# Pooled attention by head: scores in quarters of the PE, products with V in blocks of 48 queries

## The chip, the cores and the metric

The kernel runs on one core of a Trainium2 chip. The metric is the device time of one execution in microseconds; a kernel is timed in several runs, and the median stands for it. The engines of a core are PE (matrix products, results in eight banks of PSUM), DVE (vector work), ACT (scalar functions and copies), POOL, and SP, which here only issues DMAs.

## The reference

Attention in two branches, then a feed-forward network (FFN). All inputs are float32; B = 8 batches, H = 8 heads, S = 576 positions, D = 64.

```python
q_d = q.reshape(B, H, Sd, factor, D).mean(axis=3)      # factor 4, Sd = 144; k_d, v_d alike
out_d = sm_attn(q_d, k_d, v_d)                         # softmax(scale * q k^T) v, the pooled branch
out_up = np.repeat(out_d, factor, axis=2)
mask = np.abs(pos[:, None] - pos[None, :]) < factor    # the local branch: 3 neighbours to each side
...
out_local = np.matmul(attn, v)
x = out_up + out_local                                 # (B, S, 512)
...
xn = (x - mu) / np.sqrt(var + 1e-06) * g_ln
out = x + np.maximum(xn @ w_ch1, 0.0) @ w_ch2          # 512 -> 2048 -> 512
```

The change lies in the pooled branch: for each batch and head, 144 pooled queries against 144 pooled keys, of 64 numbers each.

## The kernel before

**Tiling.** The FFN goes through the 8 x 576 = 4608 rows in 18 chunks of 256, each in 8 parts (`ffn`): line 1048 multiplies up into `h`, line 1071 multiplies down into `acc`, with ACT (`hh`) and DVE (`hl`) between. Each float32 operand there is a sum of two rounded halves, so that one product is three matmuls in the fast float32 form. The attention products are plain float32: each matmul leaves two records in the profile, a turn (transpose) one.

**Local branch** (`local`): windows of 58 rows; scores at lines 573 and 587 in 64x64 quarters of the PE, weights turned at line 622, products with V at line 643 in quarters too.

**Pooled branch** (`pooled_half`, `pooled_pair`): for each batch two halves of four heads, in each two pairs of heads (`pr`); 32 pairs in all. The first batch's pairs (`own`, `b < NPB`) get their pooled queries and keys from another path (`own_half`, line 428 turns them; `arrange`); the other 28 pairs go through `turn_qk`. A pair takes these steps, whose tile names the profile shows:

- `turn_qk` (line 791, PE, tile `gq`): the two heads' pooled queries and keys, 72 groups at a time, are turned so that the 2 x 64 numbers of the heads lie on 128 partitions.
- `turn_qk_out` (lines 800 and 804, ACT): the queries are copied into `qbdg`, a block-diagonal tile: for each block of 48 queries 96 columns, head 0's in the upper 64 partitions and head 1's in the lower, zeros elsewhere. The keys go to `ktg` as they are.
- `scores` (line 818, PE, `gs`): three matmuls, one for each block of 48 queries; thanks to the zeros one matmul does both heads, 96 rows of scores.
- `largest` (lines 822 and 823, DVE, `gmx`) and `exps` (line 831, ACT, `ag`): softmax's maximum and exponentials, three of 96x144.
- `turn_a` (line 837, PE, `gt`): the weights are turned, two tasks (`kh`, halves of 72 keys) of three turns; `turn_a_out` (line 847, ACT, `agt`) puts them in order by head.
- `times_v` (line 854, PE, `gv`): eight matmuls of 72 queries by 65 columns (V and a column of ones, whose product is softmax's sum), accumulated over the key halves.
- `divided` (lines 861 to 871, DVE) and `keep` (line 877, SP): division, and one DMA for the pair into `ud` in DRAM, from where the rows come back repeated (`load_up`).

**What sets the order.** Nothing is scheduled on the chip. Every step is a task of `Plan` with an engine, an assumed duration, the tasks it waits for, a due time, and what it takes and gives back: work units of SBUF ("u", 88 of them), PSUM banks ("a", 8) and staging buffers. `Plan.order` plays the tasks through with these numbers and writes the instructions of each engine in the order that results; on the chip each engine works through its list in that order. `CHUNK` is the planner's assumed pace of a chunk, and the due times of all branches hang on it. So attention work of later batches stands in PE's list between FFN groups, and an assumed duration changes the order alone.

Of the kernel before, what the change touches and what calls it, by code (L numbers as in the profile page):

```python
# [9 lines left out]
F32 = mybir.dt.float32  # L10
# [3 lines left out]
AF = mybir.ActivationFunctionType  # L14
# [125 lines left out]
def attention_then_ffn(  # L140
# [72 lines left out]
    qbdg = [const.tile([P, 3, 2 * GB], F32, name=f"qbdg{i}") for i in range(2)]  # L213
# [3 lines left out]
    for t in qbdg:  # L217
        nc.vector.memset(t, 0.0)
# [54 lines left out]
    CHUNK = 56  # L273
# [459 lines left out]

    def pooled_half(b, hg):
# [44 lines left out]
    def pooled_pair(b, hg, pr, x, ready):  # L779
# [5 lines left out]
        bd, vd = qbdg[pr], vds[hg]  # L785
# [11 lines left out]
        def turn_qk_out():  # L797
            for h2 in range(2):
                hs = slice(64 * h2, 64 * h2 + 64)
                nc.scalar.copy(  # L800
                    bd[hs, :, h2 * GB : (h2 + 1) * GB], y.pt[hs, 0].rearrange("p (c g) -> p c g", c=3)
                )
            y.kt = work.tile([P, SD], F32, tag="ktg", bufs=2, name=f"ktg{i}_{pr}")
            nc.scalar.copy(y.kt, y.pt[:, 1])

        def arrange():
            for h2 in range(2):
                hs = slice(64 * h2, 64 * h2 + 64)
                nc.scalar.copy(
                    bd[hs, :, h2 * GB : (h2 + 1) * GB],  # L810
                    gsum[b, hg, "q"][hs, pr].rearrange("p (c g) -> p c g", c=3),
                )
            y.kt = gsum[b, hg, "k"][:, pr]

        def scores():
            y.ps = psa(f"gs{i}_{pr}")[: 2 * GB, : 3 * SD].rearrange("p (c g) -> p c g", c=3)
            for c in range(3):
                nc.tensor.matmul(y.ps[:, c], lhsT=bd[:, c], rhs=y.kt, start=True, stop=True)  # L818
# [23 lines left out]
        def turn_a_out(kh):  # L842
            if own:
                y.at[kh] = unit([GH, 2, SD], f"agt{i}_{pr}_{kh}")
            else:
                y.at[kh] = work.tile([GH, 2, SD], F32, tag=f"agt{kh}", name=f"agt{i}_{pr}_{kh}")
            nc.scalar.copy(y.at[kh].rearrange("p h (c g) -> p c h g", c=3), y.pa[kh])

        def times_v():
            y.pv = psa(f"gv{i}_{pr}")[:GH, : 4 * (D + 1)].rearrange("p (q h e) -> p q h e", q=2, h=2)  # L850
            for h2 in range(2):
                for qh in range(2):
                    for kh in range(2):
# [3 lines left out]
                        )  # L857

# [23 lines left out]
        if b < NPB:  # L882
            t = add("ACT", 0.43, arrange, ready["q"] + ready["k"] + [lastg.s[pr]], due - 8.0)
# [3 lines left out]
        t = lastg.s[pr] = add(  # L887
            "PE", 0.73, scores, (t,), due - 6.0, take=A, give=(("u", 2),) if b < NPB and pr else ()
        )
        t = add("DVE", 0.7, largest, (t,), due - 5.0)  # L890
        ex = add("ACT", 0.79, exps, (t, None if own else lastg.t), due - 5.0, take=U if own else (), give=A)
        outs = []
        for kh in range(2):
            t = lastg.t = add("PE", 0.25, lambda kh=kh: turn_a(kh), (ex,), due - 3.0, take=A,
                                give=U if own and kh else ())
            outs.append(add("ACT", act(288), lambda kh=kh: turn_a_out(kh), (t, None if own else lastg.v), due - 3.0,
                            take=U if own else (), give=A))
        t = add("PE", 1.04, times_v, outs + ready["v"], due - 1.0, take=A, give=(("u", 2),) if own else ())
        lastg.v = lastg.vd[hg] = t
        t = add("DVE", 0.68, divided, (t,), due, take=U if b < NPB and pr == 0 else (), give=A)  # L900
        od_done.append(t)
        t = add("SP", 0.42, keep, (t,), due, lag=LAT)
# [208 lines left out]
    plan.add("POOL", 2.5, make_masks, (), 0.0)  # L1111
    choice_done = plan.add("POOL", 4.0, make_choice, (), 10.0, take=U)
# [58 lines left out]
```

## Time and profile before

| what | value |
|---|---|
| median of 3 runs | 1056.92 us (1055.81 to 1063.01) |
| the profiled execution | 1053.27 us, span 1051.3 us |
| granted PE clock, mean | 0.995 |
| PE, records of pooled scores (line 818) | 192, the first at 17.3 us, the last at 872.8 us |
| PE, records of turned weights (line 837) | 192, 24.6 to 877.3 us |
| PE, records of products with V (line 854) | 512, 30.7 to 879.8 us |
| longest wait in all, ACT `hh` for PE `h` | 363.5 us in 102 waits |
| waits of PE of over 1 us in all | `gt` for ACT `ag` 3.2, `lv` for ACT `at` 2.2, `gs` for ACT `ktg` 1.6, `gs` for DVE `hl` 1.4, `lt` for ACT `la` 1.2, and 1.5 at the start |

How to read it: a row of the profile names the line, the engine, the operation, then out<-in by the program's tile names, and the shapes. For a matmul `96*72` means 96 rows (the contraction) and 72 columns of weights, and the shape behind it what streams through, as partitions x columns. "PEld" are weight loads, which the profile lists apart. Durations of matmuls are modelled up to their end and overlap one another; the starts are what the hardware recorded.

### The profile page before, as it was taken

The numbers are of one execution on the slowest core, as the hardware profiler recorded it, in microseconds if no ns is written. First come the engines' busy times: TensorE is split into PE (matmuls) and PEld (weight loads), VectorE is DVE, ScalarE is ACT, GpSimd is POOL, SyncE is SP. The second block draws the span as 40 slices with busy tenths as digits, with TensorE's granted clock in tenths as the row PEclk, the third lists the DMA queues.
The fourth block names the chain that finished last, engine by engine and source line by source line (L and its number), as shares of the span: only waits on it lengthen the run. The fifth ranks groups of instructions, "written<-read, shape, count | busy, mean of one in ns | idle before, by whom it ended". The sixth has DMA issues, their size and how long they took to land.

```text
span 1051.3 us, 24104 instructions
## 1 busy us (share of the span) xinstructions
PE 1034.3 (98%) x9450; PEld 928.9 (88%) x9450; DVE 514.0 (49%) x1301; ACT 309.8 (29%) x846; POOL 251.0 (24%) x272
## 2 busy tenths in 40 slices
PE   9999899999999999999999999999999999999998
PEld 8887798988899989989898989899989899888997
DVE  7799976343444435444434443544434444534211
ACT  6676533232212222221323222222221222221110
POOL 4213552214014320231404150141401300000000
PEclk9999999999999999999999999999999999999999
DMA  7897474434344534343434443253442443301000
GB/s 177 251 283 210 136 176 95 114 64 114 61 101 91 133 75 110 62 124 56 91 94 96 104 97 99 47 134 67 114 87 69 92 88 65 80 11 52 7 21 21
DMA packets 283702, 104.38 MB, mean 99 GB/s; under 512 B 229789, under 2 KB 270493, under 8 KB 283589
## 3 DMA queue, kind: packets, MB, share of 16 engines
q1 hardware_dynamic: 283589, 102.84, 40.8%
q8 instruction: 75, 1.23, 0.5%
q14 instruction: 38, 0.31, 0.1%
HBM read 82.58 MB, written 11.80 MB: 90 GB/s over the span
## 4 chain that ended last, share of the span: by engine, by line
PE 83%; DVE 6%; DMA 5%; SPq 2%; issue 1%; POOL 1%; ACT 1%; ACTq 0%; DVEq 0%; POOLq 0%
PE h L1048 34%; PE acc L1071 33%; PE gv L854 3%; DMA s<-in_moe_w_ch_dram 2%; PE gs L818 2%; PE lv L643 2%; PE ls L587 2%; DVE cva L370 2%; PE lt L622 1%; PE px L975 1%; PE gt L837 1%; DVE lo L383 1%; SPq L714 1%; DMA x<-xl 1%; DVE cva L367 1%
## 5 line engine op out<-in xcount | busy, mean ns | idle before, releaser
L1071 PE MATMUL acc<-hi,hl 128*128 128x512 f32 x576 | 237.2, 412 | 0.6 <-DVE hl L1059 0.5
L1071 PE MATMUL acc<-lo,hh 128*128 128x512 f32 x576 | 227.4, 395 | 0.0
L1071 PE MATMUL acc<-hi,hh 128*128 128x512 f32 x576 | 225.2, 391 | 0.0
L1059 DVE SCALAR_TENSOR_TENSOR hl<-h,hh 128x512 fp32r<-128x512 f32 x144 | 98.9, 687 | 250.7 <-ACT hh L1055 222.0
L1055 ACT ACTIVATE hh<-h 128x512 fp32r<-128x512 f32 x144 | 86.2, 599 | 430.3 <-PE h L1048 363.5
L1048 PE MATMUL h<-xh,lo 128*128 128x256 f32 x1152 | 193.6, 291 | 0.2 <-DVE lo L383 0.2
L1048 PE MATMUL h<-xh,hi 128*128 128x256 f32 x1152 | 185.2, 283 | 0.0
L1048 PE MATMUL h<-xlo,hi 128*128 128x256 f32 x1152 | 185.0, 283 | 0.0
L1048 PEld LDWEIGHTS h<-xh,lo 128*128 128x128 f32 x1152 | 169.0, 190 | 17.4 <-DVE lo L383 0.4
L1048 PEld LDWEIGHTS h<-xlo,hi 128*128 128x128 f32 x1152 | 158.9, 192 | 0.0
L1048 PEld LDWEIGHTS h<-xh,hi 128*128 128x128 f32 x1152 | 158.6, 191 | 0.0
L948 POOL TENSOR_TENSOR x<-x,up 128x512 f32<-128x512 f32 x32 | 41.2, 1287 | 386.3 <-DMA x<-xl 208.1
L1071 PEld LDWEIGHTS acc<-hi,hh 128*128 128x128 f32 x576 | 108.5, 188 | 25.0
L1071 PEld LDWEIGHTS acc<-hi,hl 128*128 128x128 f32 x576 | 109.2, 190 | 16.9 <-DVE hl L1059 1.2
L1071 PEld LDWEIGHTS acc<-lo,hh 128*128 128x128 f32 x576 | 109.5, 190 | 12.7 <-DVE lo L383 0.3
L982 ACT ACTIVATE xh<-px,gain 128x128 fp32r<-128x128 f32 x144 | 43.7, 372 | 72.7 <-PE px L975 42.4
L992 DVE SCALAR_TENSOR_TENSOR xlo<-px,gain,xh 128x128 fp32r<-128x128 f32 x144 | 43.1, 345 | 39.1 <-ACT xh L982 38.6
L1079 DVE SCALAR_TENSOR_TENSOR x<-acc,x 128x512 f32<-128x512 f32 x36 | 24.7, 689 | 39.8 <-PE acc L1071 39.8
L831 ACT ACTIVATE ag<-gs,gmx 96x144 f32<-96x144 f32 x96 | 29.0, 374 | 41.9 <-DVE gmx L823 34.4
L370 DVE SCALAR_TENSOR_TENSOR cva<-s,cva 128x256 int32<-128x256 int32 x64 | 40.0, 665 | 1.1
L854 PEld LDWEIGHTS gv<-vd,agt 72*72 72x72 f32 x512 | 37.1, 145 | 1.2
L854 PE MATMUL gv<-vd,agt 72*72 72x65 f32 x512 | 37.9, 228 | 0.0
(196 smaller groups left out, 1106.9 us busy)
## 6 DMA issues: line engine op xcount, KB each, us to landing
s<-in_moe_w_ch_dram SPq DMA_DIRECT2D x64, 256.0 KB
vwin<-in_v_dram SPq DMA_DIRECT2D x160, 64.0 KB
out_dram<-x SPq DMA_DIRECT2D x36, 256.0 KB
qr<-in_q_dram SPq DMA_DIRECT2D x264, 32.0 KB
kr<-in_k_dram SPq DMA_DIRECT2D x264, 32.0 KB
up<-ud SPq DMA_DIRECT2D x28, 256.0 KB
x<-xl SPq DMA_DIRECT2D x74, 42.0 KB
ud<-od SPq DMA_DIRECT2D x32, 72.0 KB
```

Source lines behind the costliest of these rows:

```text
L370: nc.vector.scalar_tensor_tensor(out=a, in0=x.raw[i].rearrange("p (n two) -> p n two", two=2)[:, :, 0], scalar=29, in1=a, op0=ALU.logical_ ...
L587: nc.tensor.matmul(x.ps[par][64 * h2 : 64 * h2 + 64, pr], lhsT=x.qt[hs, 2 * pr + h2], rhs=x.kt[hs, 2 * pr + h2], start=True, stop=True,)
L831: nc.scalar.activation(y.a[:, c], y.ps[:, c], AF.Exp, scale=POOLED_SCALE, bias=y.mx[:, c : c + 1])
L854: nc.tensor.matmul(y.pv[:, qh, h2], lhsT=y.at[kh][:, h2, qh * GH : (qh + 1) * GH], rhs=vd[:, kh, 2 * pr + h2], start=kh == 0, stop=kh == 1,)
L948: nc.gpsimd.tensor_add(xt[n], xt[n], x.up)
L982: nc.scalar.activation(xh[c][i][:, k, j * P : (j + 1) * P], pxt[n][:, kc], AF.Copy, scale=gain[:, kc : kc + 1])
L992: nc.vector.scalar_tensor_tensor(out=xlo[c][i][:, k, ts], in0=pxt[n][:, kc], scalar=gain[:, kc : kc + 1], in1=xh[c][i][:, k, ts].bitcast(F ...
L1048: nc.tensor.matmul(ph[c, p][:, fi], lhsT=wt[:, kc], rhs=xx[kc // 2][:, kc % 2], start=n == 0, stop=n == 3 * KC - 1)
L1055: nc.scalar.activation(hh[c, p], ph[c, p], AF.Relu)
L1059: nc.vector.scalar_tensor_tensor(out=hl[c, p].rearrange("p c t -> p (c t)"), in0=ph[c, p].rearrange("p c t -> p (c t)"), scalar=0.0, in1=h ...
L1071: nc.tensor.matmul(acc[c][j], lhsT=lt[:, fi, ts], rhs=rt, start=p == 0 and fi == 0 and n == 0, stop=p == NPR - 1 and fi == 1 and n == 2,)
L1079: nc.vector.scalar_tensor_tensor(out=x, in0=acc[c][j], scalar=1.0 + 2.0**-23, in1=x, op0=ALU.mult, op1=ALU.add)
```

## The change

For the 28 pairs outside the first batch the block-diagonal tile goes. The queries and keys of the pair are copied out together (`turn_qk_out_both`, one copy of 288 columns). Scores are made head by head (`scores_by_head`): for each of three blocks of 48 queries one matmul for each head, head 0 in the PE quarter at rows 0 and columns 0, head 1 in that at rows 64 and columns 64, each head with a PSUM bank of its own. Maximum, exponentials, turns and the copies behind them run once for each head (`largest_by_head`, `exps_by_head`, `turn_a_by_head`, `turn_a_out_by_head`), on 48 partitions at 0 or at 64. The turns of a head use the PE rows 0 to 63 or 64 to 127, all columns. The products with V (`times_v_by_third`) go by thirds of 48 queries, with head 0's results in the left column half and head 1's in the right: for head 0 64 columns of weights are loaded (the 48 and 16 of the next block), so that rows 48 to 63 of the result hold numbers too. `divided_by_third` divides 112 partitions by 3 blocks, and `keep_by_third` stores the pair with two DMAs.

The first batch keeps the old way. Its two block-diagonal tiles are no longer constants but two of the 88 work units, cleared on DVE by a task of their own and given back behind the first batch's scores. The planner's numbers for the new tasks are in the diff, and `CHUNK` is 55 instead of 56.

```diff
-    qbdg = [const.tile([P, 3, 2 * GB], F32, name=f"qbdg{i}") for i in range(2)]
+    qbdg = []
...
-    for t in qbdg:
-        nc.vector.memset(t, 0.0)
...
-    CHUNK = 56
+    CHUNK = 55
...
+    def clear_qbdg():
+        for pr in range(2):
+            qbdg.append(unit([P, 512], f"qbdg{pr}")[:, : 6 * GB].rearrange("p (c g) -> p c g", c=3))
+            nc.vector.memset(qbdg[pr], 0.0)
...
-        def turn_qk_out():
-            for h2 in range(2):
-                hs = slice(64 * h2, 64 * h2 + 64)
-                nc.scalar.copy(
-                    bd[hs, :, h2 * GB : (h2 + 1) * GB], y.pt[hs, 0].rearrange("p (c g) -> p c g", c=3)
-                )
-            y.kt = work.tile([P, SD], F32, tag="ktg", bufs=2, name=f"ktg{i}_{pr}")
-            nc.scalar.copy(y.kt, y.pt[:, 1])
+        def turn_qk_out_both():
+            y.qk = work.tile([P, 2, SD], F32, tag="ktg", bufs=2, name=f"ktg{i}_{pr}")
+            nc.scalar.copy(y.qk.rearrange("p t g -> p (t g)"), y.pt.rearrange("p t g -> p (t g)"))
+
+        def scores_by_head():
+
+            y.ps = [psa(f"gs{i}_{pr}_{h2}")[:, : 3 * SD].rearrange("p (c g) -> p c g", c=3) for h2 in range(2)]
+            for c in range(3):
+                for h2 in range(2):
+                    hs = slice(64 * h2, 64 * h2 + 64)
+                    nc.tensor.matmul(
+                        y.ps[h2][64 * h2 : 64 * h2 + GB, c], lhsT=y.qk[hs, 0, c * GB : (c + 1) * GB], rhs=y.qk[hs, 1],
+                        start=True, stop=True,
+                    )
+
+        def largest_by_head(h2):
+            hs = slice(64 * h2, 64 * h2 + GB)
+            if h2 == 0:
+                y.mx = work.tile([64 + GB, 3], F32, tag="gmx", bufs=4, name=f"gmx{i}_{pr}")
+            nc.vector.reduce_max(y.mx[hs], y.ps[h2][hs], axis=AX.X)
+            nc.vector.tensor_single_scalar(out=y.mx[hs], in_=y.mx[hs], scalar=-POOLED_SCALE, op=ALU.mult)
+
+        def exps_by_head(h2):
+            hs = slice(64 * h2, 64 * h2 + GB)
...
+            for c in range(3):
+                nc.scalar.activation(
+                    y.a[hs, c], y.ps[h2][hs, c], AF.Exp, scale=POOLED_SCALE, bias=y.mx[hs, c : c + 1]
+                )
+
+        def turn_a_by_head(h2):
+            hs = slice(64 * h2, 64 * h2 + GB)
+            y.pa = getattr(y, "pa", {})
+            y.pa[h2] = psa(f"gt{i}_{pr}_{h2}")[:GH, : 6 * GB]
+            for kh in range(2):
+                for c in range(3):
+                    n = (3 * kh + c) * GB
+                    nc.tensor.transpose(
+                        y.pa[h2][:, n : n + GB], y.a[hs, c, kh * GH : (kh + 1) * GH], ident[hs, hs]
+                    )
...
+        def times_v_by_third():
+
+
+            y.pv = psa(f"gv{i}_{pr}")[: 64 + GB, : 3 * (D + 1)].rearrange("p (c e) -> p c e", c=3)
+            for c in range(3):
+                for kh in range(2):
+                    for h2 in range(2):
+                        m = GB if h2 else 64
+                        c0 = (6 * h2 + 3 * kh + c) * GB
+                        nc.tensor.matmul(
+                            y.pv[64 * h2 : 64 * h2 + m, c], lhsT=y.at.rearrange("p h n -> p (h n)")[:, c0 : c0 + m], rhs=vd[:, kh, 2 * pr + h2],
+                            start=kh == 0, stop=kh == 1,
+                        )
...
-            t = add("ACT", 0.52, turn_qk_out, (t, lastg.s[pr]), due - 8.0, give=A)
+            t = add("ACT", 0.36, turn_qk_out_both, (t, lastg.qk.get(pr)), due - 8.0, give=A)
...
+            t = lastg.qk[pr] = add("PE", 0.4, scores_by_head, (t,), due - 6.0, take=(("a", 2),))
+            exs = []
+            for h2 in range(2):
+                t1 = add("DVE", 0.78, lambda h2=h2: largest_by_head(h2), (t,), due - 5.0)
+                exs.append(add("ACT", 1.1, lambda h2=h2: exps_by_head(h2), [t1, lastg.t] + exs, due - 5.0, give=A))
...
-        t = add("PE", 1.04, times_v, outs + ready["v"], due - 1.0, take=A, give=(("u", 2),) if own else ())
+        t = add("PE", 1.04 if own else 0.5, times_v if own else times_v_by_third, outs + ready["v"], due - 1.0, take=A, give=(("u", 2),) if own else ())
```

What this does to the order is shown at three places in PE's list, for the second pair of the first half of batch 3, counted from 0 (6_1 in the names). First the scores. Before:

```order
L1071 MATMUL acc4_1_4473<-lo2_4_1597,hh4_2_4483 128x512
L1071 MATMUL acc4_1_4473<-hi2_4_1575,hh4_2_4483 128x512
L818 MATMUL gs6_1_4642<-ktg6_1_4620,qbdg1_81 96x144 x3
L1071 MATMUL acc4_0_4472<-hi2_5_1603,hl4_2_4498 128x512
L1071 MATMUL acc4_0_4472<-lo2_5_1644,hh4_2_4483 128x512
```

and now, up to the first of the three matmuls for each head:

```order
L1123 MATMUL h4_4_4718<-xh4_1_4340,hi1_9_1839 128x256 x2
L1123 MATMUL h4_4_4718<-xlo4_0_4351,hi1_9_1839 128x256 x2
L1123 MATMUL h4_4_4718<-xlo4_1_4364,hi1_9_1839 128x256 x2
L810 MATMUL gs6_1_0_4795<-ktg6_1_4770 48x144
L810 MATMUL gs6_1_1_4796<-ktg6_1_4770 48x144
```

Three matmuls of 96 rows in one bank have become six of 48, alternating between the heads and their banks; they still stand between FFN groups. The turns of the weights, before:

```order
L622 MATMUL lt13_4685<-ident_66,la13_4654 128x128 x4
L837 MATMUL gt6_1_0_4690<-ident_66,ag6_1_4679 72x96 x3
L837 MATMUL gt6_1_1_4694<-ident_66,ag6_1_4679 72x96 x3
L1048 MATMUL h4_5_4664<-xh4_0_4175,lo1_11_2048 128x256 x2
L1048 MATMUL h4_5_4664<-xh4_1_4185,lo1_11_2048 128x256 x2
```

and now (`lt` and `lv` belong to the local branch):

```order
L620 MATMUL lt13_4863<-ident_66,la13_4851 128x128 x4
L838 MATMUL gt6_1_0_4870<-ident_66,ag6_1_4837 72x48 x6
L1123 MATMUL h4_5_4822<-xh4_0_4328,lo1_11_2096 128x256 x2
L1123 MATMUL h4_5_4822<-xh4_1_4340,lo1_11_2096 128x256 x2
L1123 MATMUL h4_5_4822<-xh4_0_4328,hi1_11_2071 128x256 x2
L1123 MATMUL h4_5_4822<-xh4_1_4340,hi1_11_2071 128x256 x2
L1123 MATMUL h4_5_4822<-xlo4_0_4351,hi1_11_2071 128x256 x2
L1123 MATMUL h4_5_4822<-xlo4_1_4364,hi1_11_2071 128x256 x2
L838 MATMUL gt6_1_1_4893<-ident_66,ag6_1_4837 72x48 x6
L641 MATMUL lv13_0_4900<-vwin1_77,at13_4889 64x65 x2
```

The two tasks of turns, which waited for the same exponentials and stood side by side, wait for a head's each; here an FFN group stands between them, as in 13 of the 28 pairs. The products with V, before, with the first two of eight matmuls:

```order
L1048 MATMUL h4_5_4664<-xh4_1_4185,hi1_11_1998 128x256 x2
L1048 MATMUL h4_5_4664<-xlo4_0_4192,hi1_11_1998 128x256 x2
L1048 MATMUL h4_5_4664<-xlo4_1_4209,hi1_11_1998 128x256 x2
L854 MATMUL gv6_1_4718<-vd0_82,agt6_1_0_4710 72x65
L854 MATMUL gv6_1_4718<-vd0_82,agt6_1_1_4714 72x65
```

and now, with the first two of twelve:

```order
L1146 MATMUL acc4_1_4554<-hi2_6_1780,hl4_3_4733 128x512
L1146 MATMUL acc4_1_4554<-lo2_6_1798,hh4_3_4716 128x512
L1146 MATMUL acc4_1_4554<-hi2_6_1780,hh4_3_4716 128x512
L906 MATMUL gv6_1_4933<-vd0_80,agt6_1_4891 64x65
L906 MATMUL gv6_1_4933<-vd0_80,agt6_1_4891 48x65
```

They too stay between FFN groups, now as alternating matmuls of 64 and 48 queries.

More of the change, by code (lines that the diff above doesn't have):

```diff
@@ L784, in pooled_pair @@
         own = b < NPB
-        bd, vd = qbdg[pr], vds[hg]
+        vd = vds[hg]
         def turn_qk():
@@ L806, in arrange, with turn_a_out_by_head @@
+        def turn_a_out_by_head(h2):
+            if h2 == 0:
+                y.at = work.tile([GH, 2, 6 * GB], F32, tag="agt", name=f"agt{i}_{pr}")
+            nc.scalar.copy(y.at[:, h2], y.pa[h2])
         def arrange():
@@ L817, in scores @@
             for c in range(3):
-                nc.tensor.matmul(y.ps[:, c], lhsT=bd[:, c], rhs=y.kt, start=True, stop=True)
+                nc.tensor.matmul(y.ps[:, c], lhsT=qbdg[pr][:, c], rhs=y.kt, start=True, stop=True)
         def largest():
@@ L842, in turn_a_out @@
         def turn_a_out(kh):
[L843 to L846, printed above, removed]
+            y.at[kh] = unit([GH, 2, SD], f"agt{i}_{pr}_{kh}")
             nc.scalar.copy(y.at[kh].rearrange("p h (c g) -> p c h g", c=3), y.pa[kh])
@@ L857, in times_v, with divided_by_third, keep_by_third @@
                         )
+        def times_v_by_third():
[9 more added lines that the diff above has]
+                        )
+        def divided_by_third():
+            r = work.tile([64 + GB, 3], F32, tag="gr", bufs=4, name=f"gr{i}_{pr}")
+            nc.vector.tensor_scalar(
+                out=r, in0=y.pv[:, :, D], scalar1=1e-9, scalar2=float(FACTOR), op0=ALU.add, op1=ALU.mult
+            )
+            nc.vector.reciprocal(r, r)
+            y.od = work.tile([64 + GB, 3, D], F32, tag="od", bufs=2, name=f"od{i}_{pr}")
+            nc.vector.tensor_mul(y.od, y.pv[:, :, :D], r.unsqueeze(2).broadcast_to([64 + GB, 3, D]))
+        def keep_by_third():
+            if b not in ud:
+                ud[b] = dram.tile([SD, DM], F32, tag="ud", name=f"ud{b}")
+            for h2 in range(2):
+                c0 = (4 * hg + 2 * pr + h2) * D
+                nc.sync.dma_start(
+                    ud[b].rearrange("(c g) e -> g c e", c=3)[:, :, c0 : c0 + D], y.od[64 * h2 : 64 * h2 + GB]
+                )
         def divided():
@@ L882, in pooled_pair @@
         if b < NPB:
[L883 removed]
+            t = add("ACT", 0.43, arrange, ready["q"] + ready["k"] + [lastg.s[pr], bd_done], due - 8.0)
         else:
             t = add("PE", 0.25, turn_qk, ready["q"] + ready["k"], due - 8.0, take=A, give=(("u", 2),) if pr else ())
[L886 to L889 removed]
@@ L890, in pooled_pair @@
-        t = add("DVE", 0.7, largest, (t,), due - 5.0)
-        ex = add("ACT", 0.79, exps, (t, None if own else lastg.t), due - 5.0, take=U if own else (), give=A)
+            t = add("ACT", 0.36, turn_qk_out_both, (t, lastg.qk.get(pr)), due - 8.0, give=A)
+        if own:
+            t = lastg.s[pr] = add("PE", 0.73, scores, (t,), due - 6.0, take=A, give=(("u", (2 if pr else 0) + hg),) if pr or hg else ())
+            t = add("DVE", 0.7, largest, (t,), due - 5.0)
+            exs = [add("ACT", 0.79, exps, (t,), due - 5.0, take=U, give=A)]
+        else:
+            t = lastg.qk[pr] = add("PE", 0.4, scores_by_head, (t,), due - 6.0, take=(("a", 2),))
+            exs = []
+            for h2 in range(2):
+                t1 = add("DVE", 0.78, lambda h2=h2: largest_by_head(h2), (t,), due - 5.0)
+                exs.append(add("ACT", 1.1, lambda h2=h2: exps_by_head(h2), [t1, lastg.t] + exs, due - 5.0, give=A))
@@ L1111, in attention_then_ffn @@
     plan.add("POOL", 2.5, make_masks, (), 0.0)
+    bd_done = plan.add("DVE", 0.6, clear_qbdg, (), 0.0, take=(("u", 2),))
     choice_done = plan.add("POOL", 4.0, make_choice, (), 10.0, take=U)
```

12 lines of the change are left out of this document (7 added, 5 removed).

## The prediction

> **What bounds the kernel now.** I read the page first: the busy shares, then the chain that ended last.
>
> ```profile
> PE 1034.3 (98%) x9450; PEld 928.9 (88%) x9450; DVE 514.0 (49%) x1301; ACT 309.8 (29%) x846; POOL 251.0 (24%) x272
> PE 83%; DVE 6%; DMA 5%; SPq 2%; issue 1%; POOL 1%; ACT 1%; ACTq 0%; DVEq 0%; POOLq 0%
> ```
>
> PE is the engine that is never done. An average can hide stages, so next I read its busy time (the number behind the comma) and the granted clock (behind the count) by stretches of 50 us.
>
> ```profile
> 100.00:150.00 50.00, 46.05 (x336) 0.97 0.62 157
> 150.00:200.00 50.00, 49.49 (x441) 1.00 0.49 115
> 200.00:250.00 50.00, 47.90 (x419) 0.97 0.40 94
> 250.00:300.00 50.00, 50.00 (x461) 1.00 0.41 80
> ...
> 850.00:900.00 50.00, 50.00 (x489) 1.00 0.36 75
> ```
>
> From 250 us on PE has work all the time at full clock; between 100 and 250 us it stands idle for 3.95 + 0.51 + 2.10 = 6.6 us. The changed work is spread over both parts, as the products with V show:
>
> ```profile
> 100.00:250.00 150.00, 8.42 (x112) 8.13 (x112) 0.98 0.50 122
> 250.00:900.00 650.00, 25.09 (x336) 24.73 (x336) 1.00 0.40 90
> ```
>
> A pair of heads has 16 records here, so 7 of the 28 changed pairs lie in the stretch with idle time and 21 where each microsecond that PE gains or loses is one of the kernel's. So the question is what a pair costs on PE, before and after.
>
> **What a pair costs PE now.** The profile models the ends of matmuls, so "busy" and mean durations overlap, and I go by starts. Each fence below is one burst of the pooled attention between FFN work (lines 1048 and 1071), in the timeline of PE: start, length, what. A record of line 1071 takes its start to the next one's, 0.23 us (231.21 to 231.44); a group of four of line 1048 takes 0.48 (247.00 to 247.48). A burst's price is the time from the start of the FFN record ahead to the second FFN row behind it, less these two.
>
> ```profile
> 257.75 0.40 PE L1071 MATMUL acc<-hi,hh 128*128 128x512 f32 x1
> 257.98 0.90 PE L818 MATMUL gs<-ktg,qbdg 128*96 128x144 f32 x6
> 258.62 0.49 PE L1071 MATMUL acc<-hi,hl 128*128 128x512 f32 x1
> 258.95 0.39 PE L1071 MATMUL acc<-lo,hh 128*128 128x512 f32 x1
> ```
> ```profile
> 231.21 0.39 PE L1071 MATMUL acc<-hi,hh 128*128 128x512 f32 x1
> 231.44 0.66 PE L837 MATMUL gt<-ident,ag 96*72 96x96 f32 x6
> 231.88 0.47 PE L1071 MATMUL acc<-hi,hl 128*128 128x512 f32 x1
> 232.19 0.39 PE L1071 MATMUL acc<-lo,hh 128*128 128x512 f32 x1
> ```
> ```profile
> 233.12 0.40 PE L1071 MATMUL acc<-hi,hh 128*128 128x512 f32 x1
> 233.35 1.19 PE L854 MATMUL gv<-vd,agt 72*72 72x65 f32 x16
> 234.36 0.72 PE L1048 MATMUL h<-xh,lo 128*128 128x256 f32 x4
> 234.91 0.64 PE L1048 MATMUL h<-xh,hi 128*128 128x256 f32 x4
> ```
>
> Scores: 1.20 - 0.46 = 0.74 us for 6 records. Turns of the weights: 0.98 - 0.46 = 0.52 for 6. Products with V: 1.79 - 0.23 - 0.48 = 1.08 for 16. Together 2.34 us.
>
> **What a split array costs.** None of these three works with the array split; the change splits it for all three, each in another way: scores in quarters of 64x64, turns in two halves of rows (64x128), products in two halves of columns (128x64). The trace has two relatives: the local scores in four quarters (line 587), and the first batch's turns in two column halves (line 428).
>
> ```profile
> 245.49 0.39 PE L1071 MATMUL acc<-hi,hh 128*128 128x512 f32 x1
> 245.81 0.69 PE L587 MATMUL ls<-lkt,lqt 64*64 64x64 f32 x32
> 246.43 0.73 PE L1048 MATMUL h<-xh,lo 128*128 128x256 f32 x4
> 247.00 0.64 PE L1048 MATMUL h<-xh,hi 128*128 128x256 f32 x4
> 247.48 0.64 PE L1048 MATMUL h<-xlo,hi 128*128 128x256 f32 x4
> ```
> ```profile
> 245.81 0.58 PE L587 MATMUL ls<-lkt,lqt 64*64 64x64 f32 x24
> ```
> ```profile
> 15.41 0.70 PE L573 MATMUL ls<-okt,oqt 64*64 64x64 f32 x32
> 16.04 0.77 PE L428 MATMUL lq<-ident,qo 80*64 80x80 f32 x16
> 16.64 0.72 PE L428 MATMUL lk<-ident,ko 80*64 80x80 f32 x16
> ```
>
> The line with x24 is the same burst, cut short by a narrower window: 8 records fewer end 0.11 us earlier. So four records run at once, and a round of four takes 0.058 us. The whole burst costs 1.51 - 0.23 - 0.48 = 0.80 us, of which 8 rounds make 0.46. The other 0.34 us is the way into the split array and back: the burst starts 0.32 after the record ahead and not 0.23, and the FFN behind it starts late and its first group takes 0.57, not 0.48. The whole-array bursts above pay nothing like it. In column halves 16 records take 0.60: rounds of two, 0.075 each. Where one split meets another (15.41 to 16.04) 0.63 passes, 0.46 of it rounds: 0.17 for the step.
>
> A rule for a record or round of this case, by rows of the weights plus moving columns: scores 128 + 144 take 0.123; turns 96 + 96, 0.087; products 72 + 65, 0.067; quarters 64 + 64, 0.058; column halves 80 + 80, 0.075. That is 0.45 to 0.49 ns for each row and column.
>
> **The change, part by part.**
> - Scores: 6 rounds of two quarters (2 heads, 3 blocks, two records for each matmul) of 64 + 144: 0.094 x 6 = 0.56 us. Before 0.74.
> - Turns: 12 records instead of 6, of 48 + 48, one head after the other, so not at once: 0.045 x 12 = 0.54. Before 0.52.
> - Products: 12 rounds of two column halves, 72 + 65: 0.067 x 12 = 0.80. Before 1.08.
> - Together 1.90 against 2.34: -0.44 us a pair, over 28 pairs -12.3 us.
> - The ways in and out. Counted over PE's whole order, it enters and leaves a split array 80 times before and 157 times after (28 bursts of scores, 28 of products, 41 of turns, some side by side), and split meets split 20 times, not once. 77 x 0.34 + 19 x 0.17 = +29.4 us.
> - Net +17.1 us, 0.61 a pair. In the 7 pairs before 250 us (4.3 us of it) PE's 6.6 us of idle time covers a part; I take half: +15.
>
> Bounds. No row shows row halves, nor column halves beside FFN work. At the low end both switch for nothing: then only the scores' 28 ways in and out count, 9.5 us, and the sum is about -3; with the scores' free too, -12. At the high end every burst stands alone and pays: 97 x 0.34 - 12.3 = +21. I take 0.34 for all, since line 587 is measured in exactly this place, between FFN work. The Trainium skill, "TensorEngine Tiling (Array Packing)", section Tiling Modes, Key Properties, says that a change of tiling mode, not of the tile alone, drains the engine; by that rule the halves pay as quarters do, which is the sum above, and the 0.34 us agrees with it. The same page's promise of up to twofold speed for dimensions up to 64 holds here inside a burst only (0.058 for four records).
>
> Off PE:
>
> ```profile
> L831 ACT ACTIVATE ag<-gs,gmx 96x144 f32<-96x144 f32 x96 | 29.0, 374 | 41.9 <-DVE gmx L823 34.4 <-PE acc L1071 7.5
> L847 ACT COPY agt<-gt 72x288 f32<-72x288 f32 x64 | 21.9, 400 | 26.5 <-PE gt L837 26.5
> L800 ACT COPY qbdg<-gq 64x144 f32<-64x144 f32 x56 | 15.3, 273 | 34.4 <-PE gq L791 34.0
> L804 ACT COPY ktg<-gq 128x144 f32<-128x144 f32 x28 | 7.8, 279 | 0.3
> L822 DVE TENSOR_REDUCE gmx<-gs 96x3 f32<-96x432 f32 x32 | 19.2, 600 | 25.6 <-PE gs L818 25.6
> L823 DVE TENSOR_SCALAR gmx<-gmx 96x3 f32<-96x3 f32 x32 | 6.9, 216 | 1.1
> ```
>
> ACT: three more exponentials a pair (+1.12), three copies (0.83) become one of 288 columns (about the 0.40 of line 847): +0.70, over 28 pairs +19 us on 309.8. DVE: a second maximum and its scaling, +0.82, +23 us on 514.0; the division's four blocks become three and I leave it. Both engines stay near a third and a half busy, so this is free as long as PE has FFN work to do meanwhile; the case where it hasn't is a rival below. The store of the pooled rows is two DMAs a pair instead of one, 28 more; SP's queue (SPq) holds 2% of the chain, and what stands behind a store there is loads planned tens of microseconds ahead: nothing, and if each held PE up by 0.1 us, 3 us, which the range has room for. The two block-diagonal tiles that become work units are cleared early on DVE, while PE is still turning the first batch (16.64 above): nothing. The chunk's pace in the planner, 55 for 56, only shifts places in the order: nothing, with a few microseconds either way.
>
> **The rivals.**
> 1. The row halves switch for free (the two heads' turns only lie on other rows). The turns' 41 bursts then save about 12 us: +17 - 12 = +5, some hidden: about 1060, no change to measure.
> 2. No half pays, nor do two quarters alone, because the price belongs to four quarters at once: the -12.3 us remains, but 7 of 28 pairs save where PE waits anyway: -9, 1048; -12 would be 1045. It ends on the other side. It decides from a price per way in and out under 12.3 / (77 + 9.5) = 0.14 us, with 0.34 measured and 0.17 where two splits meet; so I think little of it.
> 3. The column halves do not run at once: 24 records of 0.067 make 1.61 for the products, +0.80 a pair, +22: 1093. Against it: line 428 gives 0.0375 a record. The Trainium skill, "TensorE: Matmul & The Clock Gate", Part 3, The mechanism, has weight loads overlap with running matmuls only where the row group differs; column halves share their rows, so that rule speaks for this rival, and the rows of line 428 speak against the rule.
> 4. A new wait on PE. Scores hold two PSUM banks, and the second head's turns wait for six exponentials where it was three. Today such waits are rare, and cost this where they occur:
>
> ```profile
> 222.96 0.94 PE L622 MATMUL lt<-ident,la 128*128 128x128 f32 x4 [1.25 <-ACT la L617]
> 224.75 1.75 PE L818 MATMUL gs<-ktg,qbdg 128*96 128x144 f32 x6 [0.85 <-ACT ktg L804]
> ```
>
> 2.1 us once a batch, 7 batches: +15 on top, 1086.
>
> **How the numbers follow.** The sum is made against the profiled execution, 1053.3 us (span 1051.3); the runs shown have a median of 1056.9, 3.6 above it, and the prediction is for that kind of run: 1056.9 + 15 = 1072 us. Chances: the sum as it stands 0.50, with 1060 to 1081 as its own range; rival 1 0.14; rival 2 0.14; rival 3 0.06; rival 4 0.16. The range 1048 to 1087 leaves out rival 3 and part of 2 and 4. A measurement of this kernel tells about 1% from no change: below 1046.4 is faster, above 1067.5 slower. Faster: half of rival 2 and a little for the new order, 0.09. Slower: rivals 3 and 4 and seven tenths of the main case, 0.57. The same: 0.34.
>
> **What would show it.** Right: each of the three bursts starts about 0.32 after the FFN record ahead of it, and the first FFN group behind is late; scores start in close pairs, a pair every 0.09 us; a pair's bursts sum to 2.9 us against 2.34; PE still without idle time from 250 us on, its waits not longer in sum. Wrong: turns or products that follow FFN work at 0.23 or 0.12 us with nothing late behind them; or idle time of PE after 250 us ahead of turns, released by ACT; or a stretch before 250 us that got shorter by more than the bursts cost.

## The result, and the profile after

| kernel | median, us | range of runs, us | ratio to before, with 95% interval |
|---|---|---|---|
| before | 1056.37 | 1054.19 to 1063.01 | |
| changed | 1070.06 | 1063.24 to 1073.56 | 1.0131 [1.0090, 1.0172] |
| before, on a second chip | 1051.33 | 1048.11 to 1056.59 | |
| changed, on that chip (`a0_change_again` below) | 1072.66 | 1068.01 to 1072.99 | 1.0185 [1.0157, 1.0214] |

The change makes the kernel 13.7 us slower by the first pair of medians and 21.3 by the second; the intervals overlap between 1.0157 and 1.0172. The profiled execution of the changed kernel, 1063.24 us with a span of 1061.5, is its shortest, so the two profiles lie only 10.2 us of span apart.

The page of the changed kernel, busy shares and the chain that ended last:

```profile
PE 1045.3 (98%) x10020; PEld 917.9 (86%) x10020; DVE 537.0 (51%) x1349; ACT 332.7 (31%) x906; POOL 250.6 (24%) x272
PE 88%; DMA 5%; DVE 3%; SPq 2%; issue 1%; ACT 1%; POOL 0%; DVEq 0%; ACTq 0%; POOLq 0%
```

PE's busy time grew by 1045.3 - 1034.3 = 11.0 us (18.3 in `a0_change_again`, whose granted clock was lower: 0.990 where these two had 0.998 and 0.995). Its idle time, span less busy, was 17.0 and is 16.2. So the loss is work of PE, not waiting. The same stretches as before, PE alone:

```profile
100.00:150.00 50.00, 45.00 (x405) 0.97 0.53 135
150.00:200.00 50.00, 50.00 (x498) 1.00 0.50 114
200.00:250.00 50.00, 47.99 (x436) 1.00 0.53 115
250.00:300.00 50.00, 50.00 (x493) 1.00 0.37 68
...
850.00:900.00 50.00, 50.00 (x469) 1.00 0.39 77
```

As before, PE idles between 100 and 250 us and has work all the time in the later stretches shown. (The prediction had it so for all later stretches; before, PE idled for 1.4 us between 750 and 800 us, and now for 0.7 between 550 and 600.) Its waits, longest first (us in total, times, longest):

```profile
PE h L1123 <- DVE hl L1134: 2.3, 1, 2.3
PE gq L197 <- ACT ag L827: 2.2, 1, 2.2
PE lt L620 <- ACT la L615: 1.6, 1, 1.6
...
PE gs L810 <- ACT ktg L802: 1.4, 2, 1.0
```

None is new in size: the longest in sum before was 3.2 us.

Now the bursts, in PE's timeline, read as in the prediction: from the start of the FFN record ahead to the second FFN row behind, less 0.23 for a record of `acc` and 0.48 for a group of `h`. Scores:

```profile
403.07 0.40 PE L1146 MATMUL acc<-hi,hh 128*128 128x512 f32 x1
403.40 0.94 PE L810 MATMUL gs<-ktg 64*48 64x144 f32 x12
404.27 0.51 PE L1146 MATMUL acc<-hi,hl 128*128 128x512 f32 x1
404.61 0.40 PE L1146 MATMUL acc<-lo,hh 128*128 128x512 f32 x1
```

1.54 - 0.46 = 1.08 us, where it was 0.74. The turns, one head alone, and both heads side by side at another place:

```profile
417.44 0.64 PE L1123 MATMUL h<-xlo,hi 128*128 128x256 f32 x4
418.01 0.45 PE L838 MATMUL gt<-ident,ag 48*72 48x48 f32 x6
418.39 0.75 PE L1123 MATMUL h<-xh,lo 128*128 128x256 f32 x4
418.97 0.64 PE L1123 MATMUL h<-xh,hi 128*128 128x256 f32 x4
```
```profile
105.97 0.39 PE L1146 MATMUL acc<-hi,hh 128*128 128x512 f32 x1
106.29 0.57 PE L838 MATMUL gt<-ident,ag 48*72 48x48 f32 x12
106.79 0.50 PE L1146 MATMUL acc<-hi,hl 128*128 128x512 f32 x1
107.13 0.40 PE L1146 MATMUL acc<-lo,hh 128*128 128x512 f32 x1
```

1.53 - 0.96 = 0.57 us for one head's turns and 1.16 - 0.46 = 0.70 for both, where both were 0.52. The products with V:

```profile
422.27 0.40 PE L1146 MATMUL acc<-hi,hh 128*128 128x512 f32 x1
422.60 0.91 PE L906 MATMUL gv<-vd,agt 72*64 72x65 f32 x24
423.44 0.74 PE L1123 MATMUL h<-xh,lo 128*128 128x256 f32 x4
424.02 0.64 PE L1123 MATMUL h<-xh,hi 128*128 128x256 f32 x4
```

1.75 - 0.71 = 1.04 us, where it was 1.08. All four bursts start some 0.09 us late (0.32 or 0.33 behind `acc`, 0.57 behind `h`), and the FFN behind them is late too: 0.34 us pass from its first record to its second where 0.23 is usual, and 0.58 for 0.48. Of these two signs only the late start ahead tells the kernels apart. Behind the whole-array bursts shown in the prediction the FFN was nearly as late (0.33, 0.31 and 0.55 us), although the prediction says that they pay nothing like it. The same, as medians over the bursts that stand alone between FFN records after 60 us, worked out from the starts in the trace: scores 0.73 before and 1.06 now, turns 0.52 and 0.57 for one head or 0.70 for both, products 1.08 and 1.03.

Two of these bursts once more, cut short by a narrower window, as the prediction did with line 587:

```profile
403.40 0.45 PE L810 MATMUL gs<-ktg 64*48 64x144 f32 x4
```
```profile
422.60 0.60 PE L906 MATMUL gv<-vd,agt 72*64 72x65 f32 x13
```

Scores: eight records, four rounds of two, take 0.94 - 0.45 = 0.49, so a round is 0.122 us. Products: eleven records take 0.31, so two take 0.056. By the starts in the trace, a head's six turns alone follow one another by 0.042 us. The twelve of both heads at 106.29 are not one such row: their starts fit two rows of six, the second beginning 0.12 us after the first, so all twelve start within 0.37 us, where a head's six alone (418.01) take 0.24.

### The profile page after: what moved, and what is told of

It reads as the page before. It is cut to its first block, busy times and chain, and to the rows that moved or that the text cites. A ratio compares the mean times of both kernels' runs of the same rounds, so it can differ in the third digit from the quotient of the medians.

```text
span 1061.5 us, 25439 instructions
## 1 busy us (share of the span) xinstructions
PE 1045.3 (98%) x10020; PEld 917.9 (86%) x10020; DVE 537.0 (51%) x1349; ACT 332.7 (31%) x906; POOL 250.6 (24%) x272
## 4 chain that ended last, share of the span: by engine, by line
PE 88%; DMA 5%; DVE 3%; SPq 2%; issue 1%; ACT 1%; POOL 0%; DVEq 0%; ACTq 0%; POOLq 0%
PE h L1123 37%; PE acc L1146 35%; PE lv L641 2%; PE gs L810 2%; PE gv L906 2%; PE ls L585 2%; PE lt L620 2%; PE gt L838 1%; PE px L1050 1%; DMA s<-in_moe_w_ch_dram 1%; DMA x<-xl 1%; DVE cva L368 1%; PE ex L1011 1%; DVE cva L365 1%; DMA qo<-in_q_dram 1%
## 5 line engine op out<-in xcount | busy, mean ns | idle before, releaser
L827 ACT ACTIVATE ag<-gs,gmx 48x144 f32<-48x144 f32 x168 | 50.9, 369 | 46.3 <-DVE gmx L820 43.3
L819 DVE TENSOR_REDUCE gmx<-gs 48x3 f32<-48x432 f32 x56 | 33.8, 604 | 30.4 <-PE gs L810 29.4
L591 DVE TENSOR_TENSOR ls<-ls,mask 128x256 f32<-128x256 f32 x66 | 26.5, 425 | 26.3 <-PE ls L585 26.2
L1037 POOL TENSOR_TENSOR mv<-mv,neg_half 128x1 f32<-128x1 f32 x36 | 20.1, 559 | 75.0 <-DVE mv L1034 62.4
```

Source lines behind the costliest of these rows:

```text
L591: nc.vector.tensor_add(x.ps[n], x.ps[n], mask.unsqueeze(1).broadcast_to([P, NPAIR, 64]))
L819: nc.vector.reduce_max(y.mx[hs], y.ps[h2][hs], axis=AX.X)
L827: nc.scalar.activation(y.a[hs, c], y.ps[h2][hs, c], AF.Exp, scale=POOLED_SCALE, bias=y.mx[hs, c : c + 1])
```

## The experiments

Each kernel is the kernel before or the changed one with one edit; a ratio is to the kernel before on the same chip. `e1` to `e7` and `a0` test steps of the prediction; `b1`, `b2` and `b3` look for a gain.

**What a trip costs.** `e1_empty_switches` is the kernel before with 84 trips into the split array that do nothing: one small matmul in a quarter ahead of scores, turns and products of each of the 28 pairs. It writes columns of a bank that nobody reads.

```diff
+    def quarter(p):
+        nc.tensor.matmul(p[:64, 448:456], lhsT=ident[:64, :64], rhs=ident[:64, :8], start=True, stop=True)
...
         def scores():
-            y.ps = psa(f"gs{i}_{pr}")[: 2 * GB, : 3 * SD].rearrange("p (c g) -> p c g", c=3)
+            p = psa(f"gs{i}_{pr}")
+            if not own:
+                quarter(p)
+            y.ps = p[: 2 * GB, : 3 * SD].rearrange("p (c g) -> p c g", c=3)
```

> The kernel before, with one more tiny matmul (64x64 of weights, 8 columns, in one quarter of the PE, two records) ahead of the scores, of the turns and of the products with V in each of the 28 changed pairs: 84 trips into the split array and back, with next to no work in them, in the same order of everything else. If the trips carry the cost, at about 0.28 to 0.34 us each with their records, the time rises by 24 to 29 us to about 1082. If they are free and the change was slower by its order or its waits, it stays within 3 us of before.

Measured: 1077.25 us against 1053.86, ratio 1.0219 [1.0177, 1.0261]. That is 23.4 us for 84 trips, 0.28 each (0.22 to 0.33 by the interval). Its page, and one trip in PE's timeline:

```profile
PE 1059.3 (99%) x9618; PEld 939.7 (88%) x9618; DVE 514.1 (48%) x1301; ACT 310.3 (29%) x846; POOL 251.6 (23%) x272
```
```profile
258.86 0.40 PE L1083 MATMUL acc<-hi,hh 128*128 128x512 f32 x1
259.19 0.28 PE L729 MATMUL gs<-ident 64*64 64x8 f32 x2
259.40 0.98 PE L824 MATMUL gs<-ktg,qbdg 128*96 128x144 f32 x6
260.12 0.49 PE L1083 MATMUL acc<-hi,hl 128*128 128x512 f32 x1
260.45 0.40 PE L1083 MATMUL acc<-lo,hh 128*128 128x512 f32 x1
```

PE is 25.0 us busier (0.30 for a trip) and idle for 13.7 instead of 17.0; the other engines hardly differ. Two records of 8 columns turn a burst of 0.74 into 1.59 - 0.46 = 1.13. By the medians of bursts that stand alone, a trip adds 0.38 us ahead of scores, 0.33 ahead of turns and 0.36 ahead of products, its two small records included.

That is more than 0.28. PE's records stand in the same order in this trace and in the one before, so the delay between the two can be read place by place. From 291 to 751 us of the kernel before, 44 trips delay PE by 15.7 us, 0.36 each. The 25 trips ahead of that delay it by 2.3 us only: in that part PE has idle time, and the granted clock between 100 and 150 us and between 200 and 250 was 1.00 in this execution and 0.97 in the one before. So 0.28 is what the whole time shows of a trip, and 0.36 what it costs where PE is never idle.

So the price belongs to the change of the array and not to the work done there. An equally small matmul in the whole array was not run for comparison; that the whole-array scores cost their six records and no more (6 x 0.122 = 0.73 us) speaks against a price for any change of task.

`e7_empty_halves` does the same with halves: 28 trips into a row half ahead of the scores, 28 into a column half ahead of the products.

```diff
+    def row_half(p):
+        nc.tensor.matmul(p[:, 448:456], lhsT=ident[:64], rhs=ident[:64, :8], start=True, stop=True)
+
+    def column_half(p):
+        nc.tensor.matmul(p[:64, 448:456], lhsT=ident[:, :64], rhs=ident[:, :8], start=True, stop=True)
```

> The kernel before with 56 trips with next to no work in them: 28 into row halves ahead of the scores (64 rows, all columns), 28 into column halves ahead of the products with V. Order unchanged. If halves cost what a quarter's trip cost (23.4 us for 84, 0.28 each), +15.6 us: 1065 to 1070. If one kind of half is free, +8; if both are, 1051 to 1055.

Measured: 1071.22 against 1053.77, ratio 1.0171 [1.0124, 1.0218]: 17.4 us for 56 trips, 0.31 each (0.23 to 0.41), a little above what was expected. One trip into a row half:

```profile
260.32 0.40 PE L1083 MATMUL acc<-hi,hh 128*128 128x512 f32 x1
260.64 0.39 PE L729 MATMUL gs<-ident 64*128 64x8 f32 x2
260.96 0.98 PE L827 MATMUL gs<-ktg,qbdg 128*96 128x144 f32 x6
261.68 0.49 PE L1083 MATMUL acc<-hi,hl 128*128 128x512 f32 x1
262.01 0.40 PE L1083 MATMUL acc<-lo,hh 128*128 128x512 f32 x1
```

1.69 - 0.46 = 1.23 us for a burst of 0.74. By the same medians as above, row halves add 0.48 us and column halves 0.36, so neither kind is free, which the average alone does not say. The row half's small records have 128 columns of weights and start 0.13 us apart, where the quarter's, with 64, start 0.08 apart; that is part of its higher price.

**Undoing one part.** `e6_whole_scores` is the changed kernel with the scores of both heads in one whole-array matmul again, from a block-diagonal tile with head 1's columns at 64, and with maximum and exponentials for both heads at once; turns and products stay split.

```diff
-            t = lastg.qk[pr] = add("PE", 0.4, scores_by_head, (t,), due - 6.0, take=(("a", 2),))
+            t = lastg.qk[pr] = add("PE", 0.73, scores_both, (t,), due - 6.0, take=A)
...
+        def scores_both():
+            y.ps = psa(f"gs{i}_{pr}")[: 64 + GB, : 3 * SD].rearrange("p (c g) -> p c g", c=3)
+            for c in range(3):
+                nc.tensor.matmul(y.ps[:, c], lhsT=bds[pr][:, c], rhs=y.kt, start=True, stop=True)
```

> The changed kernel with the scores undone: block-diagonal tile of 112 columns, whole array, one bank, maximum and exponentials for both heads at once; turns in row halves and products in column halves stay as in the change. PE's sum by measured bursts is 13 us under the changed kernel: about 1058 to 1061. If the scores had only the price I gave them (0.90 us a pair against 0.74), the gain is 5 to 8 us: 1062 to 1066.

Measured: 1061.62 against 1053.86, ratio 1.0081 [1.0052, 1.0110], 0.6 us above the one range that was expected and 0.4 below the other. Between 38% and 56% of the change's loss is gone (0.81% left of 1.31 or 1.85). Its scores' burst is back at 0.73 by the same median, but PE's idle time is 1060.5 - 1038.7 = 21.8 us, and one wait alone is

```profile
PE lt L623 <- ACT la L618: 6.1, 1, 6.1
```

where the longest in sum was 2.3 in the changed kernel: a wait that the new order brought. Not all of the gain is the scores': both heads' turns now wait for the same exponentials and stand side by side in all 28 pairs, so the turns are 28 bursts instead of 41.

`e2_whole_turns` is the changed kernel with the turns of both heads in the whole array: six records for a pair, of 112 rows.

```diff
-        def turn_a_by_head(h2):
-            hs = slice(64 * h2, 64 * h2 + GB)
+        def turn_a_both(kh):
...
+            for c in range(3):
+                nc.tensor.transpose(
+                    y.pa[kh][:, c, : 64 + GB], y.a[:, c, kh * GH : (kh + 1) * GH], ident[: 64 + GB, : 64 + GB]
+                )
```

> The changed kernel with one part undone: the turns of the weights take both heads at once in the whole array (6 records of 112 columns instead of 12 of 48, and the rows between the heads, 48 to 63, are zeros). If row halves pay for their way in and out like quarters, PE saves about 5 us (27 ways in fewer, at the end 0.6 us a pair against 0.7 where the two bursts stood side by side and 1.14 where not): about 1065. If row halves switch for free: no gain, about 1070, or slower because both heads' exponentials are now waited for.

Measured: 1073.17, ratio 1.0177 [1.0139, 1.0214]: no gain that can be told, where about 1065 was expected if row halves pay. The turns of both heads now cost 0.59 us by the same median, where they cost 0.70 side by side and 2 x 0.57 apart, so the saving is there burst by burst. PE's busy time does not show it: 1047.6 us lies between the two executions of the change (1045.3 and 1052.6). PE waits 19.1 us of the span (1066.7 - 1047.6) where it waited 16.2 and 17.8. One wait alone, again on the order, is 4.0:

```profile
PE lt L622 <- ACT la L617: 4.0, 1, 4.0
```

The turns' share of the whole time is not shown by this run.

`e3_scores_only` leaves only the scores split: turns and products as before the change.

```diff
-        t = add("PE", 1.04 if own else 0.5, times_v if own else times_v_by_third, outs + ready["v"], due - 1.0, take=A, give=(("u", 2),) if own else ())
+        t = add("PE", 1.04, times_v, outs + ready["v"], due - 1.0, take=A, give=(("u", 2),) if own else ())
```

> As the last, and the products with V undone too (whole array, 72 queries by 72 keys, one store a pair): of the change only the scores in quarters, head by head, with their maxima and exponentials, are left. PE's sum by measured bursts is +11.6 us on before (scores 1.06 us a pair against 0.73) and 7 us under the changed kernel: about 1064 to 1067. If the products or the turns carried the loss, this is back at before, 1057.

Measured: 1085.52, ratio 1.0278 [1.0241, 1.0315], slower than the whole change. All theories missed it. `e3b_scores_only` is the same kernel, planned with 1.06 us for the split scores and a pace of 56:

```diff
-    CHUNK = 55
+    CHUNK = 56
...
-            t = lastg.qk[pr] = add("PE", 0.4, scores_by_head, (t,), due - 6.0, take=(("a", 2),))
+            t = lastg.qk[pr] = add("PE", 1.06, scores_by_head, (t,), due - 6.0, take=(("a", 2),))
```

> As the run with the scores alone in quarters, but planned with 1.06 us for them and the pace of before (56). PE's sum is +10.8 us on before. If that run's 1085 was waits of its order, this comes to 1062 to 1068. If the scores in quarters themselves bring the waits, it stays over 1075.

Measured: 1064.89 against 1051.33, ratio 1.0123 [1.0094, 1.0151], inside what was expected. The two kernels compute the same with the same tiles, so the 1.5% between them comes with the order and the pace. The granted clock was lower too: 0.984 to 0.987 in the runs of `e3`, 0.993 to 0.997 in those of `e3b`; whether the order brought that is not shown. In `e3b` most of the loss is the scores': PE is busy for 1042.1 us where it was 1034.3, the split scores cost 1.06 us a pair for 0.73, which is 28 x 0.33 = 9.2 us of the 13.6 between the medians, and the turns of 112 columns 0.59 for 0.52, another 2.0.

**The planner's numbers.** The same chip ran `a0_change_again`, the changed kernel unaltered, to see how firm the first result is.

> The changed kernel unaltered, for a comparison on the chip of the next three: 1.009 to 1.017 times before by all theories.

Measured: 1072.66 against 1051.33, ratio 1.0185 [1.0157, 1.0214], a little above what was expected. Its profiled execution has a span of 1070.4 us, 8.9 above the first one, with the same bursts to 0.01 us. The stretches show where it lost them, first this execution and then the shorter one:

```profile
0.00:50.00 50.00, 47.08 (x787) 0.93 0.79 195
...
100.00:150.00 50.00, 44.28 (x376) 0.93 0.46 124
...
200.00:250.00 50.00, 47.49 (x452) 0.93 0.53 115
```
```profile
0.00:50.00 50.00, 47.65 (x812) 1.00 0.83 203
```

It gets through 25 records fewer in the first 50 us at a granted clock of 0.93, and the clock is 0.93 again between 100 and 150 us (0.97 in the shorter one) and between 200 and 250 (1.00). Record for record, it is 4.2 us behind at 35 us, 5.9 at 187 and 9.1 at 262, and from there on the distance stays at 8.9 to 9.2 to the end: the difference between these two executions lies in the head of the kernel, not in the bursts.

`e4_chunk56` sets the pace back to 56, `CHUNK = 56`.

> The changed kernel at the pace of before (56 for 55): the order alone. PE's bursts sum to 2 us more. If the pace is nothing, 1066 to 1076; if the change lives or dies by it, more than 10 us off that.

Measured: 1067.18 against 1053.77, ratio 1.0134 [1.0091, 1.0176]: no difference that can be told, as the prediction had it.

`e5_true_costs` tells the planner what the bursts really take.

```diff
-            t = lastg.qk[pr] = add("PE", 0.4, scores_by_head, (t,), due - 6.0, take=(("a", 2),))
+            t = lastg.qk[pr] = add("PE", 1.06, scores_by_head, (t,), due - 6.0, take=(("a", 2),))
...
-            t = lastg.t = add("PE", 0.25, lambda kh=kh: turn_a(kh) if own else turn_a_by_head(kh), exs if own else [exs[kh]], due - 3.0, take=A,
+            t = lastg.t = add("PE", 0.25 if own else 0.57, lambda kh=kh: turn_a(kh) if own else turn_a_by_head(kh), exs if own else [exs[kh]], due - 3.0, take=A,
...
-        t = add("PE", 1.04 if own else 0.5, times_v if own else times_v_by_third, outs + ready["v"], due - 1.0, take=A, give=(("u", 2),) if own else ())
+        t = add("PE", 1.04 if own else 1.03, times_v if own else times_v_by_third, outs + ready["v"], due - 1.0, take=A, give=(("u", 2),) if own else ())
```

> The changed kernel with the planner told what its trace measured: scores 1.06 us a pair instead of 0.4, a head's turns 0.57 instead of 0.25, products 1.03 instead of 0.5. Only the order changes. If the loss is PE's own work, this stays within 5 us of the change (1065 to 1075; the new order's bursts sum to 2.5 us less). If the loss came from planning with numbers that are too low, it falls to 1060 or less.

Measured: 1095.60, ratio 1.0411 [1.0382, 1.0440], a miss for every theory. The waits of PE:

```profile
PE px L1050 <- DVE xn L1041: 12.2, 3, 6.9
PE lt L620 <- ACT la L615: 5.0, 1, 5.0
PE gv L906 <- DVE hl L1134: 3.2, 1, 3.2
```

These three are 20.4 us, and PE is idle for 1093.2 - 1055.3 = 37.9 us in all, where the repeat was idle for 17.8; its busy time, 1055.3 us, is near the 1052.6 of the repeat. The granted clock was 0.981 to 0.988 in these runs and 0.990 to 0.995 in the repeat's. Why measured durations give an order that waits more stays open; `e3b`, where one of them helped, went the other way.

**A version that beats both.** If a trip costs 0.3 us, fewer trips should pay in the kernel before. In `b1_joined` the products with V of one local window and the scores of the next one, both in quarters, are one task of PE for 32 windows, so that trips fall from 80 to 48. `b2_joined55` is the same with `CHUNK` 55; `b3_joined_lag` the same as `b1` with the planner's assumed delay from a task to those that wait for it at 0.8 us for 0.6; the first part of the edit below belongs to `b3` alone.

```diff
-        self.lags = (80, 0.3, 0.6)
+        self.lags = (80, 0.3, 0.8)
...
+        def joined(fn, turned, due2, give):
...
+            def both():
+                times_v()
+                fn()
+
+            tv = add("PE", 1.25, both, [at, vt] + turned, due - 1.0, take=(("a", 4),), give=(("u", 1 + give[0][1]),))
```

> The kernel before, with the local branch's products with V of one window and the scores of the next (both in quarters) in one task of PE from window 7 on, so that they share a trip: 80 trips become 48, with the same matmuls. If a trip costs 0.28 to 0.34 us here too, PE needs 10 us less: 1044 to 1049. If the four PSUM banks that the joined task takes at once make PE wait, the gain is lost: 1054 or more.

Measured: 1049.26 against 1051.33, ratio 0.9972 [0.9952, 0.9992]. PE is busy for 6.5 us less than in the profile before, but idle for 22.3 us where it was 17.0, and the longest waits are

```profile
PE gs L843 <- ACT ktg L829: 4.6, 5, 2.2
PE gt L862 <- ACT ag L856: 3.7, 4, 1.9
```

where these two were 1.6 and 3.2.

> The joined local branch with a pace of 55. Its PE work is 10 us under before, and 5 us of that went into waits of PE for ACT. If those waits hang on where the tasks stand, a tighter pace may lose them: 1044 to 1048; if not, as the joined one, 0.995 to 1.0 of before.

Measured: 1055.43 against 1053.77, ratio 1.0038 [1.0006, 1.0070]: no gain.

> The joined local branch with 0.8 us instead of 0.6 assumed between a task and the one that uses its result, so that PE's tasks stand further behind what they wait for. If PE's waits for ACT come from too little room, they shrink and the time is 1044 to 1048; if not, 0.995 to 1.005 of before.

Measured: 1046.88 against 1053.77, ratio 0.9940 [0.9911, 0.9969], faster than both kernels, by 0.6% for the one before. The kernel before with the delay of 0.8 alone was not run, so it is not shown how much of this is the shared trips' and how much the order's; the same joined tasks gave 0.9972 and 1.0038 in the other two. Its page, and one joined burst in PE's timeline:

```profile
PE 1021.8 (98%) x9462; PEld 924.5 (89%) x9462; DVE 510.9 (49%) x1293; ACT 316.3 (30%) x878; POOL 250.3 (24%) x272
```
```profile
302.59 0.64 PE L1073 MATMUL h<-xlo,hi 128*128 128x256 f32 x4
303.16 0.70 PE L644 MATMUL lv<-vwin,at 64*64 64x65 f32 x32
303.67 0.65 PE L588 MATMUL ls<-lkt,lqt 64*64 64x64 f32 x32
304.25 0.74 PE L1073 MATMUL h<-xh,lo 128*128 128x256 f32 x4
304.83 0.64 PE L1073 MATMUL h<-xh,hi 128*128 128x256 f32 x4
```

64 records in quarters for 2.24 - 0.96 = 1.28 us. The prediction's burst of 32 such scores alone cost 0.80, and here 32 products and 32 scores share one trip: the scores start 0.51 behind the products, of which 8 rounds of 0.058 make 0.46, so the step between them is 0.05 at most. A joined burst costs 1.28 us where two alone cost 0.82 each. PE is busy for 12.5 us less than before and idle for 22.3 (1044.1 - 1021.8) where it was 17.0.

## Why the prediction was right

1072 us was forecast, and 1070.06 and 1072.66 were measured. The mechanism held: the loss is PE's work, in the ways in and out of the split array. The sizes of the other terms were off, and that they cancelled is luck.

| burst, its trip included | before, us | predicted, us | measured, us |
|---|---|---|---|
| scores | 0.73 | 0.56 + 0.34 = 0.90 | 1.06 |
| turns, one head | | 0.27 + 0.34 = 0.61 | 0.57 |
| turns, both side by side | 0.52 | 0.54 + 0.34 = 0.88 | 0.70 |
| products with V | 1.08 | 0.80 + 0.34 = 1.14 | 1.03 |

- **The ways in and out.** Predicted 0.34 for each kind of split. With nothing else changed, quarters cost 0.28 and halves 0.31 on average over the whole time, and 0.33 to 0.38 for quarters, 0.36 for column halves and 0.48 for row halves by their bursts. Taken from the changed kernel's bursts, as price less rounds, it is 1.06 - 6 x 0.122 = 0.33 for scores, 0.57 - 6 x 0.042 = 0.32 for a head's turns and 1.03 - 12 x 0.056 = 0.36 for products. The rule of the Trainium skill, "TensorEngine Tiling (Array Packing)", section Tiling Modes, Key Properties, that a change of mode drains the engine, agrees with all of these; the page gives no price.
- **The scores' rounds: the term that was mis-sized most.** The prediction counted rows of weights and columns, 0.094 us for 64 + 144. Measured 0.122, the same as the whole array's 128 + 144 before. The five rows that the rule was made from could not tell: in each of them the rows of weights and the columns are nearly equal in number (128 and 144, 96 and 96, 72 and 65, 64 and 64, 80 and 80). Half the rows save nothing here, so splitting the scores bought no time inside the burst (6 rounds, 0.73 us, both ways) and the whole trip is loss. 28 x 0.16 = 4.5 us more than predicted, in the sum.
- **The products' rounds** take 0.056, not 0.067: 28 x 0.11 = 3.1 us less.
- **The turns.** The prediction's "one head after the other, so not at once" does not hold: side by side the two heads' twelve records partly run at once, as their starts show, and take 0.18 us less than predicted, which 15 pairs have (2.7 us less). Alone a head's are 0.04 less, 26 times (1.0 less).
- **The sum.** All bursts together, 28 x 1.06 + 15 x 0.70 + 26 x 0.57 + 28 x 1.03 = 83.8 us against 28 x 2.33 = 65.2: +18.6, had every burst stood alone. The 20 steps from split to split, which the prediction priced at 0.17 for 0.34, take 3.4 off; three kinds of them, measured in bursts of two splits side by side, save 0.19 to 0.20 each. That leaves +15, between the 10.2 of the two profiles and the medians' 13.7 and 21.3. The prediction had +17.1 here, and came to +15 only by what it took off for idle time.
- **What hides it.** Two of the 17 us were to go under PE's idle time before 250 us. Idle time in the three stretches shown was 6.6 and is 5.00 + 0.00 + 2.01 = 7.0: nothing was hidden there that the profiles show. So the bursts came out 2 us lower than forecast and the hidden part 2 us smaller, and the two errors cancel.
- **Off PE.** ACT grew by 22.9 us (19 predicted), DVE by 23.0 (23 predicted), and PE's idle time did not grow. The copies and stores cost nothing that shows.

The rivals. Rival 1, free row halves, falls by the turns' late start behind the FFN record and by the row halves' 0.48 us in `e7`; rival 2, no price for halves or two quarters, by `e1` and `e7`, and by `e6`, which gained when the scores left their quarters. Rival 3, column halves one after the other, falls by the products' 0.056 for two records. The rule of the Trainium skill, "TensorE: Matmul & The Clock Gate", Part 3, The mechanism, by which only a differing row group lets loads overlap, speaks for that rival and does not agree with this row. Rival 4, a new wait on PE, falls for this change by its idle time and waits. In `e5` the same instructions in another order did wait, so it fell by the order that the planner happened to give, and the prediction had no means to see that.

What was not tried: the split products alone. Their price and their rounds are read from the trace, and no run separates their part of the whole time, nor that of the turns.

## What to carry to other kernels

Here each way into a split array and back costs 0.3 to 0.4 us, in quarters or halves, so a split pays only where it shortens the burst by more; half the rows of weights shortened nothing here, and joined bursts of the same split share one trip. A rule fitted to rows in which two causes move together cannot say which of them counts. Price a burst from the start of the record ahead to the second row behind, since the late neighbours are part of it. Where a planner sets the order, an assumed duration can move the time by more than the change under study, so compare PE's busy time, idle time and granted clock before blaming an operation.

## What the runs showed of the hardware

- A round's time went with the moving columns, and not with the rows of weights, in the scores: 144 columns took 0.122 us with 128 rows of weights and 96 columns of them, and with 64 rows and 48. 65 columns took 0.056 in column halves and 64 took 0.058 in quarters, all near 0.85 to 0.91 ns a column. The products before do not fit: their records of 65 columns start 0.065 us apart. They have 72 columns of weights; in the split products the records with 64 columns of weights start 0.058 apart and those with 48 0.057. Whether the columns of weights count where there are more of them was not tested.
- Bursts of the same split follow one another with a step of 0.05 us at most (products to scores in `b3`), while the way from the whole array and back costs 0.28 to 0.38, and 0.48 with the small records of the row halves.
- The granted clock was 0.93 in three stretches of the repeat in which PE idled for 2.9, 5.7 and 2.5 us, and 1.00, 0.97 and 1.00 in the same stretches of the first execution, with 2.35, 5.00 and 2.01 us idle. Two executions of one program differ by 8.9 us in span, with the same bursts; whether the idle time lowered the clock was not tested.
